# Two chunks of a retention kernel: block loads and VectorE transposes in place of plain loads and TensorE transposes

## The chip, the cores and the metric

One core of one Trainium2 chip. The metric is the device time of one execution in microseconds (us). "Span" is the length of a profiled execution, some 1.7 us less than the time that the chip reports for it.

## The reference, cut to what matters

```python
# retention: batch 4, 8 heads, 768 steps, head size 64; float32 (the weights come as float64)
state = gamma * state + k_t (outer) v_t
y_t   = (1 / sqrt(64)) * q_t @ state
# then, with x = y as 3072 tokens of 512:
h = x @ w_in                      # 512 -> 2048
g = h * erf(softplus(h))
out = g @ w_out                   # 2048 -> 512
```

## The kernel before

The kernel takes the sequence in 24 chunks of 128 steps (6 for each batch). A chunk needs its keys and queries scaled by decay factors and **transposed**, so that the scores k.q can be formed on TensorE. The dense part runs in groups: first four "plain" groups (g = 0 to 3) over the first 512 tokens, while VectorE converts the float64 weights, then 40 fast groups (from g = 4 on) with seven products in place of eight. Each group's work on the chunks stands between its products.

There are two ways to transpose. A chunk loaded plainly has three DMAs (k, q, v), one scaling on VectorE, eight transposes on TensorE into PSUM, and two copies on ScalarE. A chunk loaded in blocks (number NB or above, before: 8) has 34 DMAs, which place blocks of 32x32 so that VectorE's block transposes make the full one:

```python
def ret_scale(j):                                   # K_
    if j >= NB:
        nc.vector.tensor_tensor(KQ[j][:, 0], KQ[j][:, 0], kq_s[...], op=ALU.mult)      # L390
        for i, x in enumerate((KB[j], KQ[j][:, 1]...)):
            nc.vector.tensor_tensor(x, x, kq_b[...], op=ALU.mult)                      # L397
        return
    nc.vector.tensor_tensor(KQ[j], KQ[j], kq_s[...], op=ALU.mult)                      # L400

def ret_transpose(j):                               # T
    if j >= NB:
        for name, store, x in (("k", KT, KB[j]), ("q", QT, ...)):
            nc.vector.transpose(store[j]..., x)                                        # L410
        return
    for i, (name, store) in enumerate((("k", KT), ("q", QT))):
        p = ret_psum()
        for u in range(HP):
            nc.tensor.transpose(p[:, u, :], KQ[j][...], ident)                         # L415
        nc.scalar.copy(store[j], p)                                                    # L421
# ... cut ...
for g in range(G0, NG):                             # the fast groups
    first = g == G0
    hidden_part(g, 1); hidden_part(g, 2)            # products 1 and 2 (L719); L732 adds 2 to 1
    if first: gated(g - 1)                          # L637
    if first: T(j)                                  # chunk 6
    hidden_part(g, 6)
    if first: S_(j); M(j); K_(j + 1); block_scales()     # scores L428, mask L440, scaling of 7
    hidden_part(g, 5)                               # into the bank that L732 reads
    if first: T(j + 1)                              # chunk 7
    hidden_part(g, 7)
    if first: project(g - 1, 0)                     # L662
    # ... cut ...
```

Products 1, 2, 6, 5, 7 are written here in the order in which they run. What the texts call the "third product" is the one numbered 5, the first behind chunk 6's scores (fourth in the order of the group).

## Time and profile before

| | before |
|---|---|
| time, median of 3 runs (lowest to highest) | 690.17 us (689.99 to 691.67) |
| profiled span | 688.0 us |
| TensorE / VectorE / ScalarE busy | 678.0 / 384.0 / 257.6 us |
| TensorE idle from 135.2 to 151.4 us | 0.57 us |

How to read it: a share of busy time averages over stages with different limits.

I use one measure throughout: **the stretch**, from the start of the first product of the first fast group to the start of the projection (L662) behind it, read from the timeline of TensorE. Before: 135.03 to 147.75, 12.72 us.

### The profile page before, as it was taken

How to read it: one execution, taken by the hardware profiler on the slowest of the kernel's cores; microseconds unless marked ns; L12 is line 12 of the kernel's file. 1: busy time of each engine (PE TensorE's matmuls, PEld its weight loads, DVE VectorE, ACT ScalarE, POOL GpSimd, SP SyncE). 2: the span in 40 equal slices, each digit the busy share in tenths (PEclk: the TensorE clock that was granted, in tenths of full speed). 3: DMA queues.
4: the chain of work that ended last, by engine and by line, in shares of the span. 5: the costliest groups of instructions: out<-in, count | busy, mean ns of one | idle time of the engine just before them, and what ended most of it. 6: DMA issues, size and time to landing. Idle time of an engine off the chain costs nothing.

```text
span 688.0 us, 14344 instructions
## 1 busy us (share of the span) xinstructions
PE 678.0 (99%) x6214; PEld 577.8 (84%) x6214; DVE 384.0 (56%) x591; ACT 257.6 (37%) x293; POOL 6.6 (1%) x21
## 2 busy tenths in 40 slices
PE   8899999999999999999999999999999999999997
PEld 8544444586999999999999999999999999999996
DVE  4799999264954643653564455454544554343324
ACT  3377362425234144144242342441441432433430
POOL 2000000010000000000000000000000000000000
PEclk9999999999999999999999999999999999999999
DMA  9999963102322321322222222322222200000000
GB/s 193 212 239 243 240 193 62 28 1 44 104 39 40 75 43 35 75 33 46 64 47 44 67 41 46 71 37 44 51 60 41 48 34 1 2 32 1 1 31 32
DMA packets 147216, 47.12 MB, mean 68 GB/s; under 512 B 135760, under 2 KB 136016, under 8 KB 147152
## 3 DMA queue, kind: packets, MB, share of 16 engines
q1 hardware_dynamic: 144640, 45.66, 30.4%
q8 instruction: 49, 0.80, 0.5%
q10 hardware_dynamic: 2512, 0.53, 0.5%
q14 instruction: 15, 0.12, 0.1%
HBM read 39.86 MB, written 6.29 MB: 67 GB/s over the span
## 4 chain that ended last, share of the span: by engine, by line
PE 86%; DVE 8%; issue 2%; SPq 1%; DMA 1%; ACT 0%; DVEq 0%
PE hp L719 36%; PE o L791 36%; PE o L662 6%; PE hp L648 2%; PE r L527 1%; PE hp L492 1%; DVE w_out_sb L215 1%; DVE w_out_sb L220 1%; DMA e<-in_q_dram 1%; SPq L119 1%; DVE w_out_sb L223 1%; PE o L563 1%; DVE w_in_sb L223 1%; DVE w_in_sb L229 1%; PE hp L542 1%
## 5 line engine op out<-in xcount | busy, mean ns | idle before, releaser
L719 PE MATMUL hp<-xs,w_in_sb 128*128 128x128 f32 x1280 | 149.8, 275 | 0.0
L719 PEld LDWEIGHTS hp<-xs,w_in_sb 128*128 128x128 f32 x1280 | 147.8, 192 | 1.6 <-issue 0.5
L791 PE MATMUL o<-w_out_sb,h 128*128 128x256 f32 x640 | 141.7, 379 | 0.0
L791 PEld LDWEIGHTS o<-w_out_sb,h 128*128 128x128 f32 x640 | 121.6, 190 | 16.5
L719 PE MATMUL hp<-xT,w_in_sb 128*128 128x128 f32 x960 | 113.7, 275 | 0.0
L719 PEld LDWEIGHTS hp<-xT,w_in_sb 128*128 128x128 f32 x960 | 111.9, 192 | 1.9 <-issue 1.0
L791 PE MATMUL o<-w_out_sb,e 128*128 128x256 f32 x480 | 112.1, 383 | 0.0
L637 DVE TENSOR_TENSOR e<-h,e 128x1024 f32<-128x1024 f32 x42 | 49.6, 1222 | 102.7 <-ACT e L618 102.7
L791 PEld LDWEIGHTS o<-w_out_sb,e 128*128 128x128 f32 x480 | 88.2, 190 | 11.6
L648 PE MATMUL hp<-xT,w_in_sb 128*128 128x512 f32 x128 | 56.6, 595 | 0.8 <-DVE w_in_sb L229 0.7
L744 DVE TENSOR_TENSOR h<-h,hp 128x512 f32<-128x512 f32 x20 | 13.8, 688 | 75.3 <-PE hp L719 75.3
L608 ACT ACT_TABLE_LOAD x24 | 30.8, 1283 | 61.1 <-issue 45.4
L648 PEld LDWEIGHTS hp<-xT,w_in_sb 128*128 128x128 f32 x128 | 23.8, 190 | 29.8 <-issue 27.3
L618 ACT ACTIVATE e<-e 128x2048 f32<-128x2048 f32 (+1 forms) x23 | 42.1, 1836 | 0.2
L608 ACT ACTIVATE e<-h 128x2048 f32<-128x2048 f32 x22 | 42.0, 1910 | 0.2
L732 DVE TENSOR_TENSOR h<-h,hp 128x512 f32<-128x512 f32 x20 | 13.8, 688 | 49.6 <-PE hp L719 49.6
L742 ACT COPY h<-hp 128x512 f32<-128x512 f32 x20 | 11.7, 586 | 60.2 <-PE hp L719 60.2
L737 ACT COPY h<-hp 128x512 f32<-128x512 f32 x20 | 11.7, 587 | 57.9 <-PE hp L719 57.9
L735 ACT COPY h<-hp 128x512 f32<-128x512 f32 x20 | 11.7, 586 | 55.3 <-PE hp L719 55.3
L618 ACT ACT_TABLE_LOAD x24 | 30.8, 1283 | 0.4
L581 ACT COPY xT<-r 128x256 f32<-128x256 f32 x32 | 10.4, 375 | 54.8 <-PE r L527 54.8
L730 ACT COPY h<-hp 128x512 f32<-128x512 f32 x20 | 11.8, 588 | 48.3 <-PE hp L719 48.3
(134 smaller groups left out, 674.1 us busy)
## 6 DMA issues: line engine op xcount, KB each, us to landing
w_out_sb<-in_moe_w_out_dram SPq DMA_DIRECT2D x14, 512.0 KB, 5.7
w_in_sb<-in_moe_w_in_dram SPq DMA_DIRECT2D x12, 512.0 KB, 12.0
kq<-in_k_dram SPq DMA_DIRECT2D x23, 256.0 KB, 3.5
v<-in_v_dram SPq DMA_DIRECT2D x23, 256.0 KB, 3.1
out_dram<-r SPq DMA_DIRECT2D x23, 256.0 KB, 3.3
kq<-in_q_dram SPq DMA_DIRECT2D x256, 16.0 KB, 1.8
kb<-in_k_dram SPq DMA_DIRECT2D x256, 16.0 KB, 1.7
w_out_sb<-in_moe_w_in_dram SPq DMA_DIRECT2D x4, 512.0 KB, 10.3
```

The costliest lines, as they stand in the source:

```text
L223: nc.vector.scalar_tensor_tensor(power, hi, 1 << 31, power, op0=ALU.bitwise_and, op1=ALU.bitwise_or)
L608: nc.scalar.activation(E[g], HS[g], AF.Softplus)
L618: nc.scalar.activation(E[g][:, half], E[g][:, half], AF.Erf)
L637: nc.vector.tensor_tensor(E[g][:, half], HS[g][:, half], E[g][:, half], op=ALU.mult)
L648: nc.tensor.matmul(p, w_in_of(ft, kk), XC[0][:, kk, :], start=(kk == 0), stop=(kk == n_k - 1))
L662: nc.tensor.matmul(O[0][tt].rearrange("p (d c) -> p d c", d=2), E[g][:, u * TCH + tt * P : u * TCH + (tt + 1) * P], w_out_of(ft), start=(f ...
L719: nc.tensor.matmul(bank[:, u, :], w_in_sb[:, s, IN[a], kk, u * P : (u + 1) * P], XS[m][b][:, kk, :], start=(p in (1, 2, 5) and u == 0 and ...
L730: nc.scalar.copy(h["11"], flat)
L732: nc.vector.tensor_tensor(h["11"], h["11"], flat, op=ALU.add)
L735: nc.scalar.copy(h["12"], flat)
L744: nc.vector.tensor_tensor(h["12"], h["12"], flat, op=ALU.add)
L791: nc.tensor.matmul(O[m][i][:, half, :], G[g][a][:, u * P : (u + 1) * P], w_out_sb[:, s, OUT[b], u, :], start=i not in started, stop=(s == ...
```

## The change

Its intent: take the 16 transposes of chunks 6 and 7 off TensorE, which is the bound there, and give them to VectorE, which is idle for 14 us just ahead. For that both chunks have to be loaded in blocks, and the decay factors in block order (the block scales, 17 tiny DMAs) are needed earlier; they are issued ahead of the last weights.

```diff
-    NB = 2 * JPC
+    NB = JPC + 2
@@ work of plain groups 2 and 3, as (at once, waiting) for each quarter
-            ([(O_, 4), (load, 6)], [(A, 4)]),
-            ([(T, 5), (load, 7)], []),
+            ([(O_, 4)], [(A, 4)]),
+            ([(T, 5)], []),
             ([(S_, 5)], [(M, 5)]),
-            ([(O_, 5)], [(A, 5)]),
+            ([(O_, 5), (load_block_scales,)], [(A, 5)]),
         ],
         [
-            ([(load_block_scales,)], []),
+            ([(load, 6)], []),
+            ([(load, 7)], []),
             ([], [(x_sums, G0)]),
-            ([(load, 8)], [(K_, 6)]),
-            ([], []),
+            ([], [(block_scales,)]),
         ],
@@ the projections of plain group 2
+                elif g == G0 - 1 and tt == 0:
+                    waiting.extend([(K_, JPC + 2), (T, JPC + 2)])
+                elif g == G0 - 1 and tt == 1:
+                    load(JPC + 4)
+                elif g == G0 - 1 and tt == 3:
+                    K_(JPC + 3)
+                    T(JPC + 3)
@@ first fast group: T(j), K_(j + 1), block_scales() and T(j + 1) removed
```

More of the change, by code (lines that the diff above doesn't have):

```diff
@@ L915 @@
                 put_part(put, step)
-        if first:
-            T(j)
         hidden_part(g, 6)
@@ L921 @@
             M(j)
-            K_(j + 1)
-            block_scales()
         for _ in range(2):
@@ L931 @@
         hidden_part(g, 5)
-        if first:
-            T(j + 1)
         hidden_part(g, 7)
```

## The prediction

> **What bounds the kernel now.** I read the page's busy shares first, then the table of waits, then the chain that ended last in order of time, and last the timelines of TensorE, VectorE and the DMA queue in the stretch that the change touches. The times on the chip were 689.99, 690.17 and 691.67 us, and the profiled span is 688.0.
>
> Busy shares on the page:
>
> ```profile
> PE 678.0 (99%) x6214; PEld 577.8 (84%) x6214; DVE 384.0 (56%) x591; ACT 257.6 (37%) x293; POOL 6.6 (1%) x21
> ```
>
> TensorE is busy for 678 of 688 us. But the average hides two stages. In a table by stretch, VectorE is busy for 54.25 of the 55 us from 38 to 93 us, where it converts the weights, and there the chain runs through VectorE. From 93 us on the chain is TensorE almost without a break. The change touches the border of plain group 3 and the first fast group (g = 4), from about 76 to 160 us. The chain there (start, us, what):
>
> ```profile
> 121.45 13.73 PE o L662 x32
> 135.19 3.57 PE hp L719 x32
> 138.76 0.87 PE r L415 x8
> 139.63 1.79 PE hp L719 x16
> 141.42 1.09 PE r L428 x16
> 142.51 1.98 PE hp L719 x16
> 144.49 0.57 issue
> 145.06 1.06 PE r L415 x8
> 146.13 1.79 PE hp L719 x16
> 147.91 3.44 PE o L662 x8
> ```
>
> L415 is the transpose on TensorE (chunk 6 at 138.76, chunk 7 at 145.06), L719 the products of the fast group, L428 the scores of chunk 6, L662 the projection of the plain group. All 16 transposes lie on the chain, and so does the only gap, 0.57 us. The chain calls it "issue", but the timeline of VectorE shows what comes just before its end:
>
> ```profile
> 138.87 0.69 DVE L732 TENSOR_TENSOR h<-h,hp 128x512 f32<-128x512 f32 x1 [14.18 <-PE hp L719]
> 139.47 2.35 DVE L637 TENSOR_TENSOR r<-h,r 128x1024 f32<-128x1024 f32 x2
> 142.54 1.29 DVE L440 TENSOR_TENSOR am<-r,causal 128x512 f32<-128x512 f32 x2 [0.72 <-PE r L428]
> 143.75 1.22 DVE L400 TENSOR_TENSOR kq<-kq,kq_s 128x1024 f32<-128x1024 f32 x1
> ```
>
> The mask (L440) and then the scaling of chunk 7 (L400) end at about 144.9, and its transposes start at 145.06. I read the gap as a wait for that scaling; that is my inference from the times. The 14.18 us of idle VectorE ahead of L732 are the room the change uses.
>
> The DMA queue of SyncE, which issues nearly all loads, looks like this there (start, us occupied by issuing):
>
> ```profile
> 90.18 1.51 SPq L172 DMA_DIRECT2D w_in_sb<-in_moe_w_out_dram  x2
> 99.93 0.88 SPq L172 DMA_DIRECT2D w_out_sb<-in_moe_w_out_dram  x2
> 100.86 8.59 SPq L347 DMA_DIRECT2D kq_b<-decay_k_dram  x16
> 109.50 0.43 SPq L351 DMA_DIRECT2D by_b<-decay_s_dram  x1
> 110.03 0.38 SPq L113 DMA_DIRECT2D kq<-in_k_dram  x1
> 110.45 7.70 SPq L95 DMA_DIRECT2D kq<-in_q_dram  x16
> 118.20 7.54 SPq L95 DMA_DIRECT2D kb<-in_k_dram  x16
> 125.84 0.38 SPq L122 DMA_DIRECT2D v<-in_v_dram  x1
> ```
>
> One chunk in blocks (chunk 8 here, L113 to L122) holds the queue for 126.22 - 110.03 = 16.2 us. A plain load of chunk 6 or 7 is three issues.
>
> **What the Trainium skill says.** "VectorE: DVE Perf Modes", section "The three transpose paths": VectorE transposes only 32x32 blocks, TensorE a full 128x128. Hence the block loads, where the DMA places the blocks so that the 32x32 transposes make the full one. The trace agrees as far as it goes: the later chunks use block loads and stream transposes of 702 and 667 ns, each for a whole 128x512 tile. "TensorE: Matmul & The Clock Gate", "Part 4: PE-mode transpose": about 275 ns for a transpose in a kernel, into PSUM, so that a copy must follow. The trace shows 272 ns for one, and copies of 590 ns on ScalarE; but back to back they cost the chain only 0.87/8 = 0.11 us each. "Perfetto Trace Analysis", "DMA Instruction — HWDGE": a DMA issue's record ends when the sequencer is free, and the movement of the data is outside it. So I add the time to landing to every issue: the trace has 1.6/1.7/4.4 us (least, median, most) for the blocks. "GPSIMD Engine Reference", "1. Specifications", has GpSimd share its SBUF interfaces with VectorE when VectorE reads two SBUF inputs. Of the five small GpSimd products of the block scales the trace has durations of 242 ns to 1183 ns (3.37 us in all, beside VectorE sums), so I allow 1.2 us for the first.
>
> **The change part by part.** The order of instructions by engine (built, not run) shows these moves.
>
> 1. TensorE loses 16 transposes and gains nothing. Before, from 135.19 to 147.91 there are 12.72 us. What must stay is 3.57 (two products) + 1.79 + 1.09 (scores) + 1.79 + 1.79 = 10.03. The middle product counts 1.79, not 1.98, since the extra 0.19 is the tail of its last matmul, seen only because a gap follows. Saved: 12.72 - 10.03 = 2.69 us. By terms: 0.87 for chunk 6; 1.06 + 0.57 + 0.19 = 1.82 for chunk 7 with its wait. All of it is on the chain.
>
> 2. ScalarE loses four copies of 0.59 us = 2.4 us. It was waiting for TensorE there; nothing is gained by that alone.
>
> 3. VectorE loses two scalings of 1.22 us, and gains for each chunk three half-size products (0.68 each) and two transposes (0.70 and 0.67). In the trace of chunk 8 these five run from 157.86 to 160.97, that is 3.1 us. Two chunks are 6.2 us, plus 0.4 for the block scales, which move forward. The new work stands ahead of L732 in VectorE's order. The last conversion ends at 124.7 before. So scales and chunk 6 can run from 124.7 to about 128.3. Chunk 7 stands behind it and needs its load.
>
> 4. The DMA queue. The block scales now stand ahead of the last weight piece. Without the plain loads of chunks 6 and 7 (5.6 us and 5.3 us of queue time at 77.4 to 83.0 and 84.9 to 90.1, mostly waiting), the preceding weights issue no later than at 90.18, so the 17 scale issues (about 9.1 us) run in the queue's wait until 99.93, when the last weight piece's buffer comes free. That piece then goes out at 99.9 to 101. Chunk 6 in blocks follows at about 101 to 117, chunk 7 at 117 to 133.3, chunk 8 at 133.3 to 149.5. Add 1.8 us for landing.
>
> 5. So chunk 7 has landed at about 135, and its scaling and transposes end at about 135 + 2.5 to 3.1 = 137.5 to 138.1. L732 waits for TensorE until 138.76 anyway. It is hidden, though by only 0.7 to 1.3 us. What TensorE itself would feel comes later: the third product after chunk 6's scores adds into the bank that L732 reads. In the new order it can begin at 135.19 + 3.57 + 1.79 + 1.09 = 141.6. L732 takes 0.69, so chunk 7 may end as late as 140.9 without a stall. The slack is about 3 us.
>
> 6. Chunk 8 is loaded 23 us later than before, by about 151.3. It is scaled at 157.86 - 2.7 = 155.2. The slack is 4 us. The gated product (L637, 2.35 us) ends at 141.8, ahead of its projection at 145.2. The mask of chunk 6, 141.7 to 143, is needed at 152.2.
>
> Sum: -2.69 us on the chain, +0 from the rest. From 151 us on TensorE runs without a wait that ends later than its own work, so the saving is carried to the end. 690.17 - 2.69 = 687.48, say 687.5 us (0.39%).
>
> **The rivals.** A: the block loads of chunk 7 come too late. The two loads together hold the queue for 32.4 us, issued one by one. If each were as slow as the slowest seen (2.08 us for one issue), or the scales held the weights back by several us, VectorE would stand before chunk 7 past 140.9, and TensorE would wait at the third product. For it speaks the queue, full from 101 to 149; against it the steady rate (the 16 later chunks have a median of 0.43 us per issue). A delay of 3 us in the loads costs nothing, 5 us costs 2 of the 2.69: 689.5. B: VectorE becomes the bound. Against it: busy for 3.19 of the 13.7 us from 121.5 to 135.2, and the added work is 6.6. If it delayed the conversion of the last weights the projection of group 3 would wait, but that piece ends at 124.7 and is needed at 145. I give this 1 in 25; cost up to 2 us. C: the gap is not the scaling but another wait, such as the scores' PSUM pair coming free at the mask's end (143.8). Then removing the transposes still removes it, as no other instruction there takes that PSUM before 152; so C leaves the time as predicted. D: the scales' tiny transfers, now beside weight transfers, delay a weight piece needed on VectorE's full stretch up to 123: the pieces' median landing is 5.7 us, and the last but one has from 91.7 to 103 before it is read. About 1 us of loss at most.
>
> **Range and chances.** The working figure is 687.5. A gain of 0.5 us more is possible if the fewer loads at 77 to 90 help the weights; A, B or D take back 1 to 2. The three runs before spread by 1.7 us, mostly upward. So 686.7 to 689.0. To be faster by over 2% it would need 13.8 us, five times what lies there; to be slower by over 2% the loads would have to be late by 17 us.
>
> **What would show it.** Right: L415 has gone from the chain between 135 and 151; the fast group's first products follow each other without a gap; the projection at L662 starts at about 145.2; chunk 7's transposes on VectorE end between 137 and 139, L732 starts at about 138.8, the DMA queue issues chunk 7's last block by 133, and the span is about 685.3. Wrong: a wait of TensorE for L732 before the third product, the last weight piece issued well after 101, L732 held behind L410 beyond 140.9, or a VectorE wait for a weight DMA between 98 and 115.

## The result

The changed kernel took 687.18 us in the median of 4 runs (686.69 to 687.64), against 690.08 us (4 runs) of the kernel before. The ratio is 0.9953, with a 95% interval of 0.9936 to 0.9971: faster by 0.5%, clear of the noise. Ratios here are the mean time of one kernel's runs over that of the other's in the same rounds, so they are not quite the ratio of the quoted medians. The span is 685.5 us, 2.5 less. The prediction was right: 687.5 us, with a range of 686.7 to 689.0. The medians differ by 2.90 us, more than the 2.50 us found below; the runs of the kernel before include some late ones (see e9 and e11), and against the median of 26 runs without those, 689.8 us, the change is about 2.6 us faster.

The page after, busy shares:

```profile
PE 676.6 (99%) x6198; PEld 576.5 (84%) x6198; DVE 388.1 (57%) x599; ACT 255.6 (37%) x289; POOL 5.7 (1%) x21
```

Sixteen TensorE instructions fewer, VectorE busier by 4 us, ScalarE less busy by 2 us. The chain that ended last (start, us, what), in the first fast group after the change:

```profile
135.55 5.36 PE hp L719 x48
140.91 1.09 PE r L428 x16
142.00 3.77 PE hp L719 x32
145.77 3.44 PE o L662 x8
```

L415 and the gap ("issue") have gone. Products and scores follow each other. The stretch in the timeline is 135.38 to 145.60 = 10.22 us, **2.50 us less** than before. The rest of the span agrees: the first product starts 0.35 us later than in the profile before (the lateness is there at 72.9 us, before the edit touches anything), and 0.35 us are made up at the very end, between VectorE's last instruction and the end of the span, for which I have no cause; 2.50 remain.

VectorE's timeline just ahead (start, us, line, what; in brackets the idle time before it and what ended it):

```profile
127.52 0.64 DVE L390 TENSOR_TENSOR kq<-kq,kq_s 128x512 f32<-128x512 f32 x1
136.85 0.69 DVE L397 TENSOR_TENSOR kb<-kb,kq_b 128x512 f32<-128x512 f32 x1 [8.70 <-DMA kb<-in_k_dram]
...
138.69 0.67 DVE L410 STREAM_TRANSPOSE qT<-kq 128x512 f32<-128x512 f32 x1
139.29 0.65 DVE L732 TENSOR_TENSOR h<-h,hp 128x512 f32<-128x512 f32 x1
```

VectorE stands for 8.70 us before chunk 7's key blocks, and the add L732 stands behind it. The add starts 3.91 us after the group's first product, against 3.84 before. It ends at 139.94, and the third product starts only at 141.93. The chain does not see it, with 2.0 us to spare. The DMA queue of SyncE shows why chunk 7 lands so late:

```profile
90.18 8.28 SPq L347 DMA_DIRECT2D kq_b<-decay_k_dram  x16
...
100.30 0.90 SPq L172 DMA_DIRECT2D w_out_sb<-in_moe_w_out_dram  x2
...
101.75 9.20 SPq L95 DMA_DIRECT2D kq<-in_q_dram  x16
110.99 7.54 SPq L95 DMA_DIRECT2D kb<-in_k_dram  x16
...
119.68 8.07 SPq L95 DMA_DIRECT2D kq<-in_q_dram  x16
127.79 7.54 SPq L95 DMA_DIRECT2D kb<-in_k_dram  x16
```

The scales fit into the wait for the weights' buffer. The loads then hold the queue until 136. The first row of chunk 6 takes 9.20 us and not 7.70; the queue's table of waits has 0.8 us there for the landing of the last weights and 1.0 us for that of chunk 6's plain key load.

### The profile page after: what moved, and what is told of

It reads as the page before. It is cut to its first block, busy times and chain, and to the rows that moved or that the text cites. A ratio compares the mean times of both kernels' runs of the same rounds, so it can differ in the third digit from the quotient of the medians.

```text
span 685.5 us, 14386 instructions
## 1 busy us (share of the span) xinstructions
PE 676.6 (99%) x6198; PEld 576.5 (84%) x6198; DVE 388.1 (57%) x599; ACT 255.6 (37%) x289; POOL 5.7 (1%) x21
## 4 chain that ended last, share of the span: by engine, by line
PE 86%; DVE 8%; DMA 2%; issue 2%; SPq 1%; ACT 0%; DVEq 0%
PE hp L719 37%; PE o L791 36%; PE o L662 6%; PE hp L648 2%; PE r L527 1%; DMA e<-in_q_dram 1%; PE hp L492 1%; DVE w_out_sb L215 1%; DVE w_out_sb L223 1%; PE o L563 1%; DMA w_out_sb<-in_moe_w_out_dram 1%; DVE w_out_sb L220 1%; DVE w_in_sb L229 1%; DVE w_in_sb L223 1%; SPq L119 1%
## 5 line engine op out<-in xcount | busy, mean ns | idle before, releaser
L719 PE MATMUL hp<-xs,w_in_sb 128*128 128x128 f32 x1280 | 149.7, 275 | 0.0
L719 PEld LDWEIGHTS hp<-xs,w_in_sb 128*128 128x128 f32 x1280 | 147.8, 192 | 1.6 <-issue 0.5
L719 PE MATMUL hp<-xT,w_in_sb 128*128 128x128 f32 x960 | 113.7, 275 | 0.0
L719 PEld LDWEIGHTS hp<-xT,w_in_sb 128*128 128x128 f32 x960 | 112.0, 192 | 1.9 <-issue 1.0
L744 DVE TENSOR_TENSOR h<-h,hp 128x512 f32<-128x512 f32 x20 | 13.8, 688 | 75.3 <-PE hp L719 75.3
L732 DVE TENSOR_TENSOR h<-h,hp 128x512 f32<-128x512 f32 x20 | 13.7, 686 | 35.7 <-PE hp L719 35.7
## 6 DMA issues: line engine op xcount, KB each, us to landing
w_in_sb<-in_moe_w_in_dram SPq DMA_DIRECT2D x12, 512.0 KB, 13.8
```

What stands on the lines that cost most here:

```text
L719: nc.tensor.matmul(bank[:, u, :], w_in_sb[:, s, IN[a], kk, u * P : (u + 1) * P], XS[m][b][:, kk, :], start=(p in (1, 2, 5) and u == 0 and ...
L732: nc.vector.tensor_tensor(h["11"], h["11"], flat, op=ALU.add)
L744: nc.vector.tensor_tensor(h["12"], h["12"], flat, op=ALU.add)
```

## The experiments

**The theory**: the gain is made of the transposes' own time on TensorE plus the wait for chunk 7's scaling; it holds only while chunk 7's load keeps ahead of the add. **The rivals**: the wait alone matters, or had another cause; the order of loads does not matter, since chunk 7 is needed only near 154 us; VectorE's added work costs time directly. Every kernel gave the right result. In the first two experiments the lines of the kernel are one higher (L720 for L719).

### e1: only chunk 6 moved

```diff
-    NB = JPC + 2
+    def blocked(j): return j == JPC + 2 or j >= 2 * JPC      # and blocked(j) for j >= NB
-                elif g == G0 - 1 and tt == 3: K_(JPC + 3); T(JPC + 3)
             S_(j); M(j)
+            K_(j + 1)
         hidden_part(g, 5)
+        T(j + 1)
```

> Only chunk 6 is loaded in blocks and transposed by VectorE; chunk 7 keeps its plain load, its scaling behind the mask and its eight transposes on TensorE. Measure: the stretch of TensorE from the first product of the first fast group to the start of the plain projection behind it (12.72 us before, 10.22 us after the whole change). Theory (the gain is the transposes' own time plus the wait ahead of chunk 7's): the stretch is 11.85 us, 0.87 less than before, and the gap ahead of chunk 7's transposes stays at about 0.6 us; time about 0.9 us below before. Rival (most of the gain came with the wait, that is, with VectorE being free earlier): the stretch stays within 0.2 us of 12.72.

The chain of e1:

```profile
143.68 1.98 PE hp L720 x16
145.66 0.64 issue
146.29 1.06 PE r L416 x8
```

The stretch was 11.92 us, 0.80 less than before (expected 0.87 less), with the gap still there at 0.64. The time does not resolve it: 690.0 us, ratio 0.9994 (0.998 to 1.0009), and three of e1's six runs had a mean clock of 0.997 or 0.998; the profiled one of them had a slow start, to which I return below.

### e2: only chunk 7 moved

```diff
-    NB = JPC + 2
+    def blocked(j): return j >= JPC + 3
-                    waiting.extend([(K_, JPC + 2), (T, JPC + 2)])
+                    waiting.append((K_, JPC + 2))
+        if first: T(j)                  # back ahead of product 6
```

> Only chunk 7 is loaded in blocks and transposed by VectorE; chunk 6 keeps its plain load and its eight transposes on TensorE. Theory (the parts add up): the stretch is 12.72 - 1.06 - 0.57 = 11.09 us, with no gap, and the time is about 1.6 us below before; together with the 0.87 of the other half that makes the 2.50 measured for the whole. Rival (the halves share a wait, so either alone gets most of it): the stretch falls to 10.5 us or less here, or the two savings sum to clearly over 2.5.

Stretch 11.09 us, exactly the sum; time 687.97 us, ratio 0.9966 (0.9952 to 0.9981). The savings of e1 and e2, 0.80 and 1.63, make 2.43 of the 2.50; the missing 0.07 is the gap that grew from 0.57 to 0.64 in e1. The halves add up, and no wait is shared.

### e3: only the wait taken away

The kernel before, with chunk 7's scaling moved into VectorE's idle time; all transposes stay on TensorE.

```diff
                 if g == 1 and tt == 1:
                     waiting.append((K_, 5))
+                elif g == G0 - 1 and tt == 0:
+                    waiting.append((K_, JPC + 3))
@@ first fast group
-            K_(j + 1)
```

> The kernel before with one move: VectorE scales chunk 7 in the last plain group, in its idle time, in place of behind the mask; all 16 transposes stay on TensorE. Theory (the 0.57 us gap ahead of chunk 7's transposes is the wait for that scaling): the gap goes, the transposes follow the product at once, and the stretch falls by 0.57 to 0.76 us, to 12.0 to 12.15 us. Rival (the gap is a wait for the PSUM pair that the mask frees, or nothing that VectorE's scaling decides): the gap stays, the stretch is 12.6 to 12.75 us.

```profile
142.90 1.98 PE hp L719 x16
144.88 0.87 PE r L415 x8
145.76 1.79 PE hp L719 x16
```

The gap is gone, so it was the wait for the scaling, as inferred. The transposes behind it take 0.87 us and no longer 1.06: the 0.19 was the restart after the gap. The product ahead of it takes 1.98 with a gap behind it and without. The stretch is 11.96, 0.76 less. The time, 689.25 us (ratio 0.9988, 0.9974 to 1.0003), is of that size but not clear of noise. So the 2.50 us are 2 x 0.87 = 1.74 for the transposes and 0.76 for the gap with its restart.

### e4: the block scales behind the last weights

```diff
-            ([(O_, 5), (load_block_scales,)], [(A, 5)]),
+            ([(O_, 5)], [(A, 5)]),
-            ([(load, 6)], []),
+            ([(load_block_scales,), (load, 6)], []),
```

> The whole change, but with the loads of the block scales issued behind the last weights, as in the kernel before. Measure: the stretch from the first product of the first fast group to the plain projection behind it (10.22 us after the change, 12.72 before). Theory (the scales go out in time in which the queue waits anyway, and VectorE stands at chunk 7's load ahead of the add that the third product needs): the two block loads start 9 us later, chunk 7 lands at about 143.4 in place of 136.85 us, the add ends at about 146.5, TensorE waits about 4.6 us ahead of the third product, the stretch is 14.8 us and the time about 691.8 us, slower than before. Rival (chunk 7 itself is needed only by its scores, near 154 us, so a later load is hidden): the stretch stays at 10.2 and the time at 687.2 us.

The time was 695.88 us, ratio 1.0076 (1.006 to 1.0091): slower than before, and by 4 us more than I expected. The timelines of VectorE and TensorE, then the table by stretch (from:to, length, busy us and instructions of PE, PEld, DVE, ACT and POOL, granted TensorE clock, share of the DMA engines, GB/s):

```profile
145.75 0.69 DVE L397 TENSOR_TENSOR kb<-kb,kq_b 128x512 f32<-128x512 f32 x1 [14.45 <-DMA kb<-in_k_dram]
```

```profile
148.89 5.61 PE L719 MATMUL hp<-xs,w_in_sb 128*128 128x128 f32 x32 [7.47 <-DVE h L732]
```

```profile
148.90:154.40 5.50, 5.50 (x33) 5.50 (x34) 5.46 (x6) 0.00 (x0) 0.00 (x0) 0.66 0.23 37
```

The mechanism is the expected one: TensorE waits for L732, which stands behind chunk 7's load. Two sizes were off. The load landed at 145.75 and not at 143.4, so the wait was 7.47 and not 4.6 us. And the two products behind the wait took 5.61 us in place of 3.84, at a **mean granted clock of 0.66**. The stretch was 19.53 = 10.22 + 7.47 + 1.77, to 0.1.

### e5: chunk 7's work behind the add

```diff
-                elif g == G0 - 1 and tt == 3:
-                    K_(JPC + 3)
-                    T(JPC + 3)
@@ first fast group
             gated(g - 1)
+            K_(j + 1)
+            T(j + 1)
```

> The whole change, with chunk 7's scaling and transposes placed on VectorE behind the add and the gating of the first fast group in place of ahead of them. Theory (the add was late by some 0.4 us, but TensorE had 2 us of slack there): the add starts at the end of the second product, about 0.3 us earlier in its stretch; the stretch stays at 10.22 us and the time within 0.3 us of the change's. Rival (TensorE did feel the late add in some way): the stretch falls below 10.1 us.

Stretch 10.22 us, time 687.14 us, ratio 0.9953 (0.9938 to 0.9969): the same as the change. The order costs nothing. As a test of the late add e5 is weak, since in the change's profile the add was only 0.07 us late (3.91 against e5's 3.84 us after the first product) and not the 0.4 us of the expectation. The repetition of the change (e11 below) is the better test: there the add starts 4.53 us after the first product, 0.69 late, and the stretch is 10.21.

### e6: late scales and chunk 7 behind

Both edits, e4's and e5's.

> Scales issued behind the last weights (as in e4) and chunk 7's work behind the add and the gating (as in e5). Theory (in e4 it is VectorE's order, not the data, that makes TensorE wait): no wait ahead of the third product, stretch 10.2 us, time about 687.2 us, although chunk 7 lands at about 143.4. Rival (the late load hurts by itself, through chunk 8's load 9 us later or the scores of chunk 7): a new gap after 150 us and a time 1 to 4 us higher.

The stretch was 10.22 us, so in e4 it is VectorE's order that hands the late load to TensorE. But the time was 690.37 us, ratio 0.9995 (0.9977 to 1.0013), not 687.2. In the timeline of TensorE the wait has moved behind the stretch:

```profile
153.65 2.05 PE L719 MATMUL hp<-xT,w_in_sb 128*128 128x128 f32 x16 [1.17 <-DVE h L739]
```

Chunk 7 landed at 146.93, and behind it on VectorE now stood the mask and the next add, L739. This cost 1.4 us (541.30 from the projection to the end, against 539.8 to 539.9 in five of the other runs). The first product of this profile also started late, at 136.88, 1.50 later than in that of the change. That is not the late loads' doing: at 89.2 us TensorE is already 1.5 us behind, before the two kernels issue anything different (the scales, at 90.2 us), and the clock there is 1.00. In the profile the two make up the whole difference, 1.4 + 1.5 = 2.9 of 690.08 - 687.16. Three of the other five runs had a mean clock of 0.998 and were not profiled; what made those slow stays open.

### e8: three pairs of transposes more

```diff
                     T(JPC + 3)
+                    for _ in range(3):
+                        # both vector transposes of chunk 7 once more
```

> The whole change, and chunk 7's two VectorE transposes done four times over (three pairs more, same result), ahead of the add. It measures the slack: the add ended at 139.94 us after the change and the third product began at 142.00, so 2.06 us. Theory: three pairs take 3 x 1.25 = 3.75 us, of which 2.06 are hidden; the stretch grows by 1.7 us to 11.9, the time by 1.7 us to about 688.9. Rival (VectorE's time adds directly once it stands ahead of TensorE): plus 3.75 us; or, if VectorE's work is hidden altogether: no change.

The stretch was 13.94, not 11.9, and the time 690.64 us, ratio 1.0003 (0.9986 to 1.002). TensorE's timeline, then the wait and what follows it by stretch:

```profile
143.29 5.20 PE L719 MATMUL hp<-xs,w_in_sb 128*128 128x128 f32 x32 [2.29 <-DVE h L732]
```

```profile
141.00:142.77 1.77, 0.00 (x0) 0.00 (x0) 1.77 (x4) 0.00 (x0) 0.00 (x0) 1.00 0.15 24
142.77:146.19 3.42, 2.90 (x13) 2.90 (x14) 3.42 (x5) 0.00 (x0) 0.00 (x0) 0.50 0.22 34
146.19:148.40 2.21, 2.21 (x22) 2.21 (x21) 2.18 (x3) 0.00 (x0) 0.00 (x0) 1.00 0.24 37
```

The three pairs took 3.56 us, the slack was 1.3 in this run, and so TensorE waited 2.29. Then again the products ran slowly, at a mean clock of 0.72 from 143.3 to 148.4 us. The sum alone would fit the rival, which asks for 10.22 + 3.75 = 13.97; only its parts speak against it: a wait of 2.29 and not of 3.6 us, and 1.36 us lost to the clock.

Cut finely, the clock has two values here, 1.00 and 0.50, and the 0.72 is their mean: it falls 1.8 us after TensorE stopped and stays at 0.50 for 3.4 us. In e4, in the same way, it is 0.50 from 145.8 to 152.65 us, 6.8 us. Both came with an idle gap. After the 0.57 us gap of the kernel before, the clock stayed at 1.00. Two of e8's six runs had a mean clock of 1.000, so the fall doesn't come every time; how long they waited is not on record.

### e10: the gap filled

e8, with chunk 6's scores computed three times over, so that TensorE works while it would wait.

```diff
             S_(j)
+            # the same eight score products twice more, into the same bank
             M(j)
```

> The kernel of e8 (three pairs more of transposes on VectorE, so that TensorE waits 2.29 us for the add ahead of its third product, after which the two products took 5.20 in place of 3.77 us at a granted clock of 0.72), and the score products of chunk 6 done three times over in that wait: about 2.1 us more of TensorE work, same result. Theory (it is the idle gap of over 2 us that costs the clock, on top of the wait itself): the wait shrinks to under 0.5 us, the granted clock stays 1.00, the two products take 3.8 us, and the stretch falls from 13.94 to about 12.5 us, although TensorE does more; time 1.2 to 1.5 us below e8's. Rival (the slow products come from VectorE's full load or from the banks they share): the products stay at about 5.2 us and the stretch at 13.9 us or more.

```profile
141.78 1.96 PE L933 MATMUL r<-qT,kT 64*128 64x128 f32 x32
144.03 3.84 PE L719 MATMUL hp<-xs,w_in_sb 128*128 128x128 f32 x32 [0.30 <-DVE h L732]
```

TensorE does 2 us more work, and the stretch falls from 13.94 to 12.37 us; the products are back at 3.84. The median time is 689.28 us, 1.4 below e8's (ratios to before 0.9987 and 1.0003, in different rounds and with intervals that overlap, so the stretch carries this and not the time). VectorE was as busy as in e8. So in these two profiles it is the idle gap that lowers the clock, and the penalty comes on top of the wait.

### e7: one pair more

The same edit as e8 with one pair, 1.18 us.

> The whole change, with chunk 7's two VectorE transposes done twice (one pair, 1.19 us by e8, more ahead of the add). Theory (TensorE has 1.3 to 2.1 us of slack ahead of the third product): the add ends at most as late as the scores, the stretch is 10.2 to 10.4 us, time as after the change. Rival (VectorE's time ahead of the add adds to TensorE's at once): stretch 11.4 us or, with a fall of the clock, more.

This missed, and the rival's figure, 11.4, came true: the stretch was 11.45 us, with a wait. But its reason, that VectorE's time always adds at once, does not follow, since the slack was gone in this execution. VectorE first, then TensorE:

```profile
139.50 0.69 DVE L397 TENSOR_TENSOR kb<-kb,kq_b 128x512 f32<-128x512 f32 x1 [10.68 <-DMA kb<-in_k_dram]
```

```profile
143.82 3.84 PE L719 MATMUL hp<-xs,w_in_sb 128*128 128x128 f32 x32 [1.16 <-DVE h L732]
```

In this execution chunk 7 landed at 139.50 us, 2.65 later than in the profile of the change, while the first product started only 0.67 later. Without the extra pair the add would have ended at 142.59, and the third product was due at 136.05 + 6.55 = 142.60: no slack at all. So the slack is no constant of the kernel; it is the difference of two chains, the DMA queue's and TensorE's. Worked out in the same way it is 2.0, 1.4, 1.3, 1.5 and 0.0 us in the profiles of the change, its repetition, e8, e10 and e7. After the wait of 1.16 us the products took 3.84, without a fall of the clock. The time was 687.94 us (4 runs, 686.07 to 689.09), ratio 0.9966 (0.9948 to 0.9983).

### e9 and e11: an early gap, and the change again

The kernel before has two groups of run times. 26 of its 33 runs had a mean clock of 0.999 or 1.000 and a median of 689.8 us, and 7 had a mean clock of 0.998 and a median of 691.8 us. None of the 7 was profiled. The profile of e1 shows a slow start at 21 us. The waits of TensorE and the stretch from 21 to 27 us, in e1 and then in the kernel before:

```profile
PE r L416 <- DVE state L596: 2.2, 1, 2.2
...
21.00:27.00 6.00, 5.87 (x72) 5.18 (x72) 1.90 (x5) 1.72 (x4) 0.00 (x0) 0.72 1.11 198
```

```profile
PE r L415 <- DVE state L595: 1.4, 1, 1.4
...
21.00:27.00 6.00, 5.33 (x96) 4.32 (x96) 3.34 (x8) 2.44 (x5) 0.00 (x0) 1.00 1.09 212
```

A load that comes 0.6 us later makes the gap 2.2 in place of 1.4 us, the clock falls (to 0.50 from 22.7 to 26.1 us; the 0.72 is the mean), and all behind it is late: e1's first fast product starts 2.03 us after that of before. One spell of 3.4 us at 0.50 takes about 0.0025 off the mean clock of such a run, which is the difference between the two groups, wherever the spell lies; that it lies at this gap in the 7 late runs is inferred. e9 takes e5's order and fills the gap with four products:

```diff
+        if j + 2 == JPC:
+            keep_warm(4)               # ahead of chunk 3's transposes
```

> The order of e5, and four filler products on TensorE ahead of chunk 3's transposes near 19 us, where TensorE waits for a load: 1.44 us in the profile of the kernel before (clock stays 1.00), 2.25 us in that of e1 (clock 0.65 to 0.78 for some 6 us, and everything behind it 2 us later). Theory (the two groups of run times of one kernel, about 689.6 and 691.7 us, differ by whether that gap passes 2 us): with 0.9 us of the gap filled no run of this kernel falls in the late group, all have a mean clock of 0.999 or 1.000, and the median is 686.5 to 687.2 us. Rival (the groups have another cause): some of the 6 runs have a clock of 0.998 and are 2 us longer.

> The changed kernel unaltered, to compare with e7, e9 and e10 on the same chip. Theory: stretch 10.22 us, time about 687.2 us, or about 2 us more in those runs whose early gap passes 2 us (mean clock 0.998).

The change again (e11): stretch 10.21 us, 687.12 us, ratio 0.9956 (0.9944 to 0.9967). e9: stretch 10.22 us, 686.97 us, ratio 0.996 (0.9945 to 0.9975), a gap of 0.9 us and no run at 0.998. This agrees with the theory, but does not test it, since none of e11's five runs was at 0.998 either, and two of e9's runs took 688.4 and 689.1 us at a full clock. The second is the profiled one, and it shows another cause of a late start: at 62.7 us TensorE waits 1.30 us for the conversion of a weight piece (L229), and the first fast product starts at 137.33. So that the filler helps is not shown; nor is any version here faster than the change. e5's order has the same time and does not hang the add on the load, and I would keep it for that.

## Why the prediction was right, point by point

- **TensorE, 2.69 us less**: 2.50 measured. The term that was mis-sized is the 0.19 us, which I took off the product ahead of the gap as a tail that only a gap shows. It stays with that product, with or without the gap (e3). The 0.19 that does go is the restart of the transposes, already inside their 1.06. Chunk 7's share is thus 1.63 and not 1.82, as e2 shows.
- **The gap is the wait for chunk 7's scaling**: inferred then, shown by e3. Rival C falls.
- **ScalarE**: 2 us less busy and no effect on the chain, as said.
- **VectorE has room**: chunk 6 ran from 124.39 to 127.58 us, predicted 124.7 to 128.3. Rival B does not appear: no TensorE wait for a conversion was added.
- **The queue**: scales at 90 to 99.7, last weights at 100.3, as predicted. The block loads were slower than the 16.2 us each: chunk 7's last key block was issued at about 135.3, where I had 133, and landed at 136.85, where I had 135. The queue had to wait for landings ahead of chunk 6. So three of the signs named as right failed: the block by 133, the transposes' end by 139 (139.36) and L732 at 138.8 (139.29). The 0.7 to 1.3 us by which chunk 7 was to be hidden from L732 were not there; the slack behind it covered that.
- **The slack**: predicted about 3 us, 2.0 in the first profile, and between 0.0 and 2.0 over five. I treated it as a number and should have asked how far the two chains vary.
- **Chunk 8**: its scaling started at 155.71 without a wait (predicted 155.2).
- **Rival A** was the right danger, and its cost was too small in the text: I counted a late load microsecond for microsecond. e4 shows that a wait can cost clock too: 7.47 us of it cost 9.31. The 17 us of lateness for a time 2% slower leave my own slack out: 13.8 + 2.69 = 16.5 us of wait is 19.5 us of lateness with a slack of 3.
- **Rival D**: no wait of VectorE for weights appears between 98 and 115 us.
- **The sum**: 687.48 predicted, 687.18 measured. The error of 0.19 in the saving is smaller than what one start differs from the next (the first fast product starts between 134.39 and 137.33 us in the thirteen profiles). That the two figures lie within 0.3 us is therefore partly luck; the stretch, 2.50 against 2.69, is what bears the prediction out.

## What to carry to other kernels

Moving work off the bound engine gave its time on the chain, plus the wait that hung on it; count each gap with its restart once. Where the work goes, place it on the new engine behind the things that the bound engine waits for, because an engine that stands at a load hands the wait on to all behind it (7.47 us in e4). When two chains meet, look at several executions before calling the distance a slack, and look at the clock behind every wait of TensorE: waits of 2.25 us and more cost more than themselves in the profiles here.

## What the Trainium skill lacked or had wrong

- "TensorE: Matmul & The Clock Gate", section "What's actually happening", gives an idle window of about 3.4 us for the fall of the clock, and the page's table "Why this matters for your kernels" warns of gaps over some 3 us. Here gaps of 2.25 us (e1, at 21 us) and 2.29 us (e8) already brought a granted clock of 0.50 for 3.4 us, while gaps of 0.57, 1.16, 1.44 and 1.56 us (e6, at 20.6 us) did not. The fall came 1.8 us after TensorE had stopped in e8, 4.4 us after in e4, and in e1 3.8 us after, when TensorE was working again; so the length of a gap alone does not say when the clock falls, and these few gaps give no exact bound. e10 shows that filling the gap with useless products gained 1.57 us of the stretch.
- The same page, "Part 4: PE-mode transpose", gives some 275 ns for a bf16 transpose in one kernel. The single record agrees (272 ns, float32), but eight in a row cost the chain 0.87 us, 0.11 each. The page has no figure for back-to-back transposes, which is the one needed to size their removal.
- "Perfetto Trace Analysis", "DMA Instruction — HWDGE", says what an issue's record covers, but has no figure for a queue that issues many small loads: here 0.43 us for one, and 16 to 18 us of queue for one chunk of 34 loads, up to 2 us of it spent waiting for earlier landings.
